# Attention ahead of a mixture of experts on one core: small steps of the attention on another engine in some groups, and another order of its steps

## The chip, the cores and the metric

One Trainium2 chip, one core of it. The metric is the device time of one execution in microseconds. The kernel before took 905.72 us (median of 3 runs, 903.4 to 906.46).

## What is computed

The reference takes q, k and v (8 batches, 12 heads, 448 tokens, 64 wide, fp32), normalizes q and k by their root mean square, and computes attention; its output is laid out as 3584 tokens of 768 and goes through a router and 8 experts of 448 tokens each:

```python
def rmsnorm(x, g):
    rms = np.sqrt(np.mean(x * x, axis=-1, keepdims=True) + 1e-06)
    return x / rms * g
q_n, k_n = (rmsnorm(q, g_q), rmsnorm(k, g_k))
scores = scale * np.matmul(q_n, k_n.transpose(0, 1, 3, 2))
scores = scores - np.max(scores, axis=-1, keepdims=True)
attn = np.exp(scores)
attn = attn / (np.sum(attn, axis=-1, keepdims=True) + 1e-09)
return np.matmul(attn, v)
...
logits = x @ w_gate
...
for e in range(E):
    mask = assigned == e
    h = np.maximum(x[mask] @ w1[e], 0.0)
    out[mask] = h @ w2[e]
```

The experts' part, with the router's choice of 448 tokens for each expert in turn, is not touched by the change.

## The kernel before

The attention works on 24 groups of 4 heads. A group is two pairs of heads; a pair's 448 tokens lie as 7 units of 128 rows (the tails of two heads share a unit). For each group the steps are:

- SyncE's queue loads q, k and v (`load_qk`, `load_v`). ScalarE squares q and k (`square`, L308), VectorE sums the squares (`sumsq`, L320). `rsqrt` makes the inverse root: a logarithm and an exponential on ScalarE (L326, L328), then one correcting step, the **root**, as four small instructions on GpSimd (L331 to L334) or three on VectorE (L337 to L339).
- `norm` (L353) scales k and q by the root, `gain` (L378) multiplies q by the gains. `hi_k` and `hi_q` (L383, L388, ScalarE) take the fp16 part, `lo_k` and `lo_q` (L417, L422) what is left, the **low part**. SyncE's queue turns both by DMA (L429), and `dup_k`, `dup_q` (L397, GpSimd) copy one half to a second tile.
- A first product of q and k (`max_score`, L536 and L539) gives scores from which VectorE takes each row's maximum (`max_reduce`, L550). `put_max` (L555, ScalarE) scales and **shifts the maxima** and puts them down as fp16; TensorE turns them (`tr_max`, L485), ScalarE copies them out (L489, tile mt), and two small DMAs (`row_max`, L496) write them as a row of q's second tile, so that the second product of q and k (`scores`, L569) already has them taken off. ScalarE makes the exponential (`exp`, L580).
- TensorE multiplies by v (`av`, `av_tail`, L604), with the row sums as a 65th column. For each pair VectorE divides (`x_norm`, L639 to L643), ScalarE and VectorE split the result in two fp16 parts (`x_hi`, L654 and L655; `x_lo`, L660 and L661). For batches 0 to 6, TensorE turns a third of it at once (`x_here`, L678) in the same bank of PSUM in which the pair's product stood, and **x's turned copy** leaves it by `x_here_out`, for which `copy` (L371) is called. The gate's products with x follow (`gate`, L741 to L750).

The product tile `po` has two banks, the first scores' ring `pm` one and the ring `psc` two buffers; who holds one keeps the next user waiting.

The order of all these steps is a list. `plan` names 2230 tasks with their engine and what each needs, and `ORDER`, a string of two characters for a task, is the order in which they are written out; each engine then works its own tasks in that order and waits at each for its inputs. Which engine takes a step is looked up by `engine` (L358) in the tables `ENG` and, for the first groups, `FIRST`. Some constants of the router (L1143) and the gate's weights (L187) are made by VectorE in between. A task of the plan that uses the memory port which VectorE and GpSimd have in common is marked so (`port`); in `part`, VectorE's tasks are, except for three names:

```python
port=queue == "D" and name not in ("ss0", "ss1", "put")
```

After the last pair of heads (about 400 us) the router finds the first expert's tokens in a chain of VectorE and TensorE steps, and from about 435 us TensorE multiplies for the experts almost without a gap.

Of the kernel before, what the change touches and what calls it, by code (L numbers as in the profile page):

```python
# [30 lines left out]
AF = mybir.ActivationFunctionType  # L31
OP = mybir.AluOpType
# [57 lines left out]
class Attention:  # L90
# [276 lines left out]
    def copy(self, e, g, o, i):  # L367
        if self.engine(e, g) == "A":
# [442 lines left out]
    def plan(self):  # L811
        plan = Plan(self.RINGS)
        add, P, US = plan.add, self.P, self.US
# [19 lines left out]
        for g in range(self.NG):  # L833
# [20 lines left out]
            for a in self.halves(g):  # L854
# [45 lines left out]
                part("put", "A", "small", self.put_max, after=[("mx", *x), ("c", "qm")], make=("top", *x), opens=[("qm", g)],  # L900
# [3 lines left out]
                add(t + P["trm"], "A", US["small"], self.tr_max, g, 1, after=[("mp", *x)], make=("mt", *x), opens=[("mt", m)],  # L904
# [58 lines left out]
        for pair in range(2 * self.NG):  # L963
# [33 lines left out]
            if b < last and self.HERE:  # L997
                add(s + P["xturn"], "T", 0.12 * len(self.HERE), self.x_here, pair, after=[("x", b, hp)], make=("th", pair), uses=[("xb", b)])
                add(s + P["xtd"], self.engine("xhere", 0), 0.15 + 0.12 * len(self.HERE), self.x_here_out, pair, after=[("th", pair)], make=("xh2", b, hp),
# [17 lines left out]
    def plan_first(self, plan, g, a, t):  # L1017
# [1023 lines left out]
```

## Time and profile before

| what | us |
|---|---|
| median of 3 runs | 905.72 (903.4 to 906.46) |
| the profiled execution's own time | 904.41 |
| its span, first to last instruction | 902.6 |
| TensorE (PE) busy in it | 863.4 |
| VectorE (DVE) busy | 628.0 |
| ScalarE (ACT) busy | 469.2 |
| GpSimd (POOL) busy | 401.6 |

PE is TensorE's matrix product, DVE is VectorE, ACT is ScalarE, POOL is GpSimd, SP is SyncE, whose queue issues most DMAs. A busy share is that of instructions in work; matmuls overlap, so a busy PE can still hide short waits. A wait is put down to the instruction that ended last before it.

### The profile page before, as it was taken

Reading aid. Unit: us, or ns where it says so; the run is one execution under the profiler, and the core shown is the slowest. Engines: PE = TensorE matmul, PEld = TensorE weight load, DVE = VectorE, ACT = ScalarE, POOL = GpSimd, SP = SyncE. Lnnn points to the kernel's source line nnn. Section 1 sums busy time; section 2 is a strip of 40 time slices with the busy share of each in tenths; the row PEclk is TensorE's granted clock in tenths of the full one; section 3 lists DMA queues with packets and bytes.
Section 4 is the critical chain, followed back from the end, with each engine's and each line's share of the span. In section 5 each row is a group of like instructions: output and inputs, shape, how many; then the busy total and the mean of one; then the engine's idle time right before and its main releaser. Section 6 shows DMA issues by size and latency. Waiting matters only on the chain.

```text
span 902.6 us, 27569 instructions
## 1 busy us (share of the span) xinstructions
PE 863.4 (96%) x11763; PEld 557.4 (62%) x11765; DVE 628.0 (70%) x1503; ACT 469.2 (52%) x739; POOL 401.6 (44%) x448
## 2 busy tenths in 40 slices
PE   5989999999999999995999999999999999999996
PEld 2467777677777777784556555565555655555553
DVE  6999888888888988737887776866768675143100
ACT  4987887688887786650434333333333333242110
POOL 7899999889998897202103021101111120200001
PEclk9999999999999999995999999999999999999998
DMA  7677999999899998424747096785929387591001
GB/s 187 145 176 150 195 194 190 207 191 203 193 197 203 174 211 136 118 49 140 259 153 258 28 280 184 207 231 168 278 67 303 114 251 222 169 246 39 27 18 44
DMA packets 253019, 153.64 MB, mean 170 GB/s; under 512 B 178654, under 2 KB 240094, under 8 KB 251872
## 3 DMA queue, kind: packets, MB, share of 16 engines
q1 hardware_dynamic: 247388, 129.39, 60.8%
q0 software_dynamic: 4704, 22.03, 7.3%
q8 instruction: 92, 1.51, 0.7%
q10 hardware_dynamic: 804, 0.46, 0.2%
q14 instruction: 31, 0.25, 0.1%
HBM read 94.43 MB, written 22.02 MB: 129 GB/s over the span
## 4 chain that ended last, share of the span: by engine, by line
PE 66%; issue 18%; DVE 5%; POOL 3%; DMA 3%; ACT 2%; SPq 1%; POOLq 0%; DVEq 0%; ACTq 0%
PE po L604 15%; PE ph L1804 15%; PE py L1821 13%; PE psc L569 12%; PE pm L539 2%; PE py L1830 2%; PE psc L539 1%; DMA qkraw<-in_q_dram 1%; POOL out_dram L1840 1%; DVE mx L550 1%; POOL rows L1737 1%; PE rp L1450 1%; DMA q<-mt 1%; PE pm L536 1%; SPq L249 1%
## 5 line engine op out<-in xcount | busy, mean ns | idle before, releaser
L1804 PE MATMUL ph<-xt,w1h 128*128 128x448 f16 (+2 forms) x804 | 209.5, 344 | 0.0
L604 PEld LDWEIGHTS po<-v,e 128*64 128x64 f32 (+1 forms) x5376 | 172.1, 138 | 41.2 <-issue 20.2
L604 PE MATMUL po<-v,e 128*64 128x65 f32 (+1 forms) x5376 | 185.8, 224 | 2.7 <-DVE xt L371 1.5
L580 ACT ACTIVATE e<-psc 128x896 f32<-128x896 f32 x168 | 151.1, 916 | 57.3 <-PE psc L569 55.8
L1840 POOL DMA_INDIRECT out_dram<-y,idx x32 | 34.3, 1073 | 280.1 <-ACT y L1823 245.7
L569 PE MATMUL psc<-q,k 128*64 128x448 f16 x1344 | 153.5, 354 | 2.1 <-POOL st L333 0.9
L1804 PE MATMUL ph<-xt,w1l 128*128 128x448 f16 (+2 forms) x402 | 135.1, 344 | 0.0
L1821 PE MATMUL py<-w2h,hl 128*128 128x384 f16 x384 | 125.0, 326 | 0.0
L1821 PE MATMUL py<-w2l,hh 128*128 128x384 f16 x384 | 125.0, 326 | 0.0
L1821 PE MATMUL py<-w2h,hh 128*128 128x384 f16 x384 | 125.0, 326 | 0.0
L1804 PEld LDWEIGHTS <-w1h 128*128 128x128 f16 x804 | 74.0, 97 | 63.8 <-issue 2.3
L550 DVE TENSOR_REDUCE mx<-pm 128x2 f32<-128x896 f32 x96 | 104.2, 1085 | 8.4 <-PE pm L539 6.0
L1792 ACT ACTIVATE hh<-ph 128x448 f16<-128x448 f32 x64 | 34.8, 543 | 144.4 <-PE ph L1804 139.6
L1821 PEld LDWEIGHTS <-hh 128*128 128x128 f16 x768 | 73.3, 97 | 46.4
L569 PEld LDWEIGHTS <-k 128*64 128x64 f16 x1344 | 73.6, 110 | 36.8 <-issue 7.5
L1823 ACT ACTIVATE y<-py 128x384 f32<-128x384 f32 x48 | 23.5, 490 | 132.6 <-PE py L1821 104.2
L1737 POOL DMA_INDIRECT rows<-xd,idx x32 | 31.8, 995 | 127.4 <-DVE idx L1631 43.2
L550 DVE TENSOR_REDUCE mx<-psc 128x2 f32<-128x896 f32 (+1 forms) x74 | 77.8, 1058 | 6.5 <-PE psc L539 5.7
L1794 DVE SCALAR_TENSOR_TENSOR hl<-ph,hh 128x448 f16<-128x448 f32 x64 | 39.2, 619 | 60.4 <-ACT hh L1792 60.2
L1724 DVE SCALAR_TENSOR_TENSOR w2l<-stage,w2h 128x768 f16<-128x768 f32 x64 | 60.1, 950 | 22.2 <-ACT w2h L1720 22.1
L1724 DVE SCALAR_TENSOR_TENSOR w1l<-stage,w1h 128x768 f16<-128x768 f32 x64 | 59.4, 950 | 3.3 <-ACT w1h L1720 3.3
L1720 ACT ACTIVATE w1h<-stage 128x1536 f16<-128x1536 f32 x32 | 47.2, 1476 | 21.4 <-DMA stage<-in_moe_w_dram 21.4
(294 smaller groups left out, 1425.3 us busy)
## 6 DMA issues: line engine op xcount, KB each, us to landing
stage<-in_moe_w_dram SPq DMA_DIRECT2D x64, 768.0 KB
vraw<-in_v_dram SPq DMA_DIRECT2D x24, 384.0 KB
xd<-xb SPq DMA_DIRECT2D x8, 1152.0 KB
qkraw<-in_q_dram SPq DMA_DIRECT2D x23, 384.0 KB
qkraw<-in_k_dram SPq DMA_DIRECT2D x23, 384.0 KB
vraw<-in_v_dram SPq DMA_DIRECT2D x24, 64.0 KB
xd<-xm SPq DMA_DIRECT2D x16, 96.0 KB
qkraw<-in_k_dram SPq DMA_DIRECT2D x22, 64.0 KB
```

The lines of the kernel that those rows point to most:

```text
L550: self.nc.vector.tensor_reduce(m, p[:, :k, :448], axis=AX.X, op=OP.max)
L569: nc.tensor.matmul(p[64 * h:64 * h + 64, i, :448], kt[:, a, n + 64 * h:n + 64 * h + 64], qt[:, a, 448 * s:448 * s + 448], start=st, stop=n ...
L580: self.nc.scalar.activation(e, p[:, :, :448], AF.Exp, scale=scale)
L604: self.nc.tensor.matmul(self.po(pair)[64 * n:64 * n + 64, w], self.T["e", d][r, i, q:q + 64], self.v1[g % 2][r, self.slot(a, u, s)], start ...
L1720: self.nc.scalar.activation(h, v, AF.Copy, scale=self.WS)
L1724: self.later(0.93, lambda w=w: self.nc.vector.scalar_tensor_tensor(l[:, w], v[:, w], self.WS, h[:, w], op0=OP.mult, op1=OP.subtract), k, i)
L1737: nc.gpsimd.indirect_dma_start(out=g[:n, c, :], out_offset=None, in_=self.xd, in_offset=bass.IndirectOffsetOnAxis(ap=idx[:n, c:c + 1], axi ...
L1792: nc.scalar.activation(hh, whole, AF.Relu)
L1794: self.later(0.6, lambda: nc.vector.scalar_tensor_tensor(hl, whole, 0.0, hh, op0=OP.max, op1=OP.subtract), k, 3.5, f)
L1804: nc.tensor.matmul(p, a[:, i, c], x[:, b, o], start=j == 0, stop=j == 17)
L1821: nc.tensor.matmul(p, a[:, f, s], b[:, f, o], start=st, stop=sp)
L1840: st = nc.gpsimd.indirect_dma_start(out=self.out, out_offset=bass.IndirectOffsetOnAxis(ap=self.router.idx[k][:n, c:c + 1], axis=0), in_=y[ ...
```

## The change

It gives eight kinds of step an engine of their own group by group: three tables of letters, one letter for each group (`ON`) or pair of heads (`XH`), are asked from group 2 on. D is VectorE, P GpSimd, A ScalarE. Counted from group 2 on: the root is VectorE's in 9 groups (3, 8, 9, 14, 16 to 19, 21), k's norm in 2 (5, 9), the gain in 3 (6, 22, 23), k's low part in 3 (10, 13, 17), q's in 1 (18); all of these were GpSimd's. The shift of the maxima (`put`) is VectorE's in 12 groups and the copy of the turned maxima (`trm`) in 4, both were ScalarE's. x's turned copy is ScalarE's for 25 of 42 pairs, and was VectorE's for all. The numbers of tasks, the buffers and all shapes stay. The order is another one from about the 60th of TensorE's blocks on; up to there it is nearly the same.

```diff
-    ENG = dict(lok="P", loq="P", dupk="P", dupq="P", normk="P", normq="P", gain="P", vfull="A", root="P", xhere="D")
+    ENG = dict(lok="P", loq="P", dupk="P", dupq="P", normk="P", normq="P", gain="P", vfull="A", root="P", put="A", trm="A")
...
+    XH = "AAAAAAAADDAAADDDDADDAADDAADDADAAAAADAAADDDDDDDDD"
+    ON = dict(root="PPPDPPPPDDPPPPDPDDDDPDPP", normk="PPPPPDPPPDPPPPPPPPPPPPPP", gain="PPPPPPDPPPPPPPPPPPPPPPDD", lok="PPPPPPPPPPDPPDPPPDPPPPPP", loq="PPPPPPPPPPPPPPPPPPDPPPPP", put="AAAADADAAADDAADDDADDDDAD", trm="AAAAAAADAAAADAAAADADAAAA")
 
     def engine(self, e, g, a=None):
+        if g >= self.EARLY and e in self.ON:
+            return self.ON[e][g]
...
-            self.nc.scalar.activation(t, self.T.pop(("mp", g)), AF.Copy)
+            self.copy("trm", g, t, self.T.pop(("mp", g)))
...
-        self.nc.scalar.activation(o, i, AF.Copy, scale=-1.0 / self.ROW, bias=math.log(self.PSC) / (scale * self.ROW))
+        m, c = -1.0 / self.ROW, math.log(self.PSC) / (scale * self.ROW)
+        if self.engine("put", g, a) == "D":
+            self.nc.vector.tensor_scalar(o, i, m, c, op0=OP.mult, op1=OP.add)
+        else:
+            self.nc.scalar.activation(o, i, AF.Copy, scale=m, bias=c)
...
-        self.copy("xhere", 0, o, self.T.pop(("th", pair)))
+        self.copy_on(self.XH[pair], o, self.T.pop(("th", pair)))
...
     ORDER = (
-        "020z0o01080706000509030+0-100A0p0q0r04111213141u1t1v1w1x1y2n2r2p2o0w2q2s0x0y3G3F0s0B151T161U1718191V1A1B1C1D"
...
+        "0z11020+120o0-13011008071u0600051t090A030p0q14161v0r04151w1U0B181x171T191y1V1A2n1B1W1C2r1D1E2p1X1F2o1Y1G1Z1K"
...
```

In the new order three places matter for what follows. In the code of the change, lines from 372 on have moved: L371 is L378, L417 L424, L397 L404, L485 L492, L550 L557, L569 L580, L604 L615, L639 to L643 are L650 to L654, L660 and L661 are L671 and L672, L1143 is L1154.

VectorE, at the gate's weights (wg), between the second pair's division and its low parts (xb, xm), which TensorE's turning waits for. Before:

```order
L643 TENSOR_TENSOR po<-po,z 128x7x64
L320 TENSOR_REDUCE st<-sq_134 128x14
L187 SCALAR_TENSOR_TENSOR wg<-wg_123,wg 128x18x8
L660 TENSOR_TENSOR xb<-po,xb 128x2x3x64
L661 TENSOR_TENSOR xm<-po,xm 128x64
```

The same place in the change:

```order
L654 TENSOR_TENSOR po<-po,z 128x7x64
L320 TENSOR_REDUCE st<-sq_134 128x14
L671 TENSOR_TENSOR xb<-po,xb 128x2x3x64
L672 TENSOR_TENSOR xm<-po,xm 128x64
L187 SCALAR_TENSOR_TENSOR wg<-wg_123,wg 128x18x8
L557 TENSOR_REDUCE mx<-pm 128x2
```

The weights went behind the two low parts; a maximum (mx) is now behind them.

VectorE, at the router's constants rankt and rankb, ahead of a turned copy (xt) that frees a bank of `po`. Before:

```order
L660 TENSOR_TENSOR xb<-po,xb 128x2x3x64
L661 TENSOR_TENSOR xm<-po,xm 128x64
L1143 CAST rankt<-rank 128x224
L1143 CAST rankb<-rank 1x8
L371 COPY xt<-po 128x2x128
L320 TENSOR_REDUCE st<-sq_134 128x14
```

In the change:

```order
L378 COPY xt<-po 128x2x128
L1154 CAST rankt<-rank 128x224
L800 TENSOR_TENSOR logits<-po,lsc 128x24
L801 TENSOR_TENSOR logits<-po,lsc 64x8
L557 TENSOR_REDUCE mx<-pm 128x2
L557 TENSOR_REDUCE mx<-psc 128x2 x2
L1154 CAST rankb<-rank 1x8
```

Both constants stand behind a turned copy now, and apart.

GpSimd, at the root of group 8 (st) and the norm of k (kn) that reads it. Before:

```order
L417 TENSOR_TENSOR ks_1841<-kn,ks_1841 128x2x7x64
L397 COPY q_1_129<-q_1347 64x896 x2
L422 TENSOR_TENSOR qs_1869<-qn,qs_1869 128x2x7x64
L331 TENSOR_TENSOR st<-st 128x28
L332 TENSOR_TENSOR st<-st 128x28
L333 TENSOR_SCALAR st<-st 128x28
L334 TENSOR_TENSOR st<-st 128x28
L353 TENSOR_TENSOR kn<-qkraw,st 128x896
```

In the change, where VectorE has that root (L337 to L339):

```order
L404 COPY q_1_129<-q_1452 64x896 x2
L424 TENSOR_TENSOR ks_1721<-kn,ks_1721 128x2x7x64
L353 TENSOR_TENSOR kn<-qkraw,st 128x896
L429 TENSOR_TENSOR qs_1897<-qn,qs_1897 128x2x7x64
L353 TENSOR_TENSOR qn<-qkraw,st 128x896
```

The four small instructions are gone from GpSimd's queue, and k's norm of group 8, which needs VectorE's root, follows a low part directly.

## Rows read from the trace of the kernel before

**Rows 1.** Busy time by stretch, all engines; columns as in its head.
```profile
core 0: us, PE busy (x) PEld busy (x) DVE busy (x) ACT busy (x) POOL busy (x), PEclk, DMA share, GB/s
...
50.00:400.00 350.00, 342.12 (x7572) 255.98 (x7569) 292.16 (x514) 269.03 (x463) 287.80 (x277) 1.00 0.89 176
...
170.62:174.03 3.41, 2.83 (x52) 2.83 (x54) 3.41 (x5) 2.30 (x8) 2.18 (x6) 0.50 1.10 191
```

**Rows 2.** Matmuls' waits, 50 to 400 us: us in total, times, longest us.
```profile
PE po L678 <- DVE xm L661: 2.0, 1, 2.0
PE po L604 <- DVE xt L371: 1.5, 2, 1.3
...
PE psc L569 <- POOL st L333: 0.9, 1, 0.9
```

**Rows 3.** Timeline, 62 to 65 us: start us, us, engine, line, operation.
```profile
62.27 2.09 POOL L378 TENSOR_TENSOR qn<-qn,gg 128x896 f32<-128x896 f32 x1
62.37 2.17 DVE L187 SCALAR_TENSOR_TENSOR wg<-wg,wg 128x144 f16<-128x144 f32 x1
...
64.45 0.55 DVE L660 TENSOR_TENSOR xb<-po,xb 128x384 f16<-128x384 f32 x1
...
65.18 0.30 PE L678 MATMUL po<-ident,xb 128*64 128x128 f16 x4 [2.02 <-DVE xm L661]
```

**Rows 4.** Timeline, 168 to 172 us, VectorE, GpSimd and the next product.
```profile
167.92 2.10 POOL L378 TENSOR_TENSOR qn<-qn,gg 128x896 f32<-128x896 f32 x1
...
168.64 1.51 DVE L1143 CAST rankt<-rank 128x224 bf16<-128x224 f32 x1
...
169.96 1.97 POOL L397 COPY q<-q 64x896 f16<-64x896 f16 x2
170.07 0.88 DVE L1143 CAST rankb<-rank 1x8 bf16<-1x8 f32 x1
...
171.20 0.70 PE L604 MATMUL po<-v,e 128*64 128x65 f32 x8 [1.28 <-DVE xt L371]
```

**Rows 5.** Groups by line and shape, 50 to 398 us: busy us, mean ns.
```profile
L378 POOL TENSOR_TENSOR qn<-qn,gg 128x896 f32<-128x896 f32 x21 | 44.0, 2097 | 1.5
L320 DVE TENSOR_REDUCE st<-sq 128x14 f32<-128x910 f32 x38 | 41.3, 1088 | 0.5 <-ACT sq L308 0.5
...
L417 POOL TENSOR_TENSOR ks<-kn,ks 128x896 f16<-128x896 f32 x21 | 39.8, 1895 | 2.7 <-ACT ks L383 1.6 <-DMA qkraw<-in_k_dram 0.6
...
L353 POOL TENSOR_TENSOR kn<-qkraw,st 128x896 f32<-128x896 f32 x20 | 33.8, 1689 | 1.0
...
L654 ACT ACTIVATE xb<-po 128x384 f16<-128x384 f32 x46 | 22.4, 487 | 6.1 <-DVE po L643 5.8
...
L371 DVE COPY xt<-po 128x256 f16<-128x256 f16 x42 | 11.9, 283 | 9.4 <-PE po L678 8.5 <-PE pm L485 0.7
...
L331 POOL TENSOR_TENSOR st<-st 128x28 f32<-128x28 f32 x20 | 4.7, 233 | 1.3 <-ACT st L328 0.9
```

**Rows 6.** The same view, 0 to 45 us, VectorE alone.
```profile
L339 DVE SCALAR_TENSOR_TENSOR st<-st 128x14 f32<-128x14 f32 x4 | 0.7, 175 | 0.1
```

**Rows 7.** Timeline, 347 to 351 us, VectorE alone.
```profile
348.34 0.86 DVE L1255 TENSOR_SCALAR keyi<-best 128x21 int32<-128x21 int32 x1
...
349.76 0.17 DVE L1257 TENSOR_SCALAR keyi<-keyi 128x21 int32<-128x21 int32 x1
```

**Rows 8.** Timeline, 378 to 383 us, TensorE around the last turning of maxima.
```profile
378.29 0.22 PE L485 MATMUL pm<-ident,qm 128*64 128x128 f16 x1
...
379.85 2.62 PE L604 MATMUL po<-v,e 128*64 128x65 f32 x84
...
382.30 1.49 PE L569 MATMUL psc<-q,k 128*64 128x448 f16 x14
```

**Rows 9.** Timeline, 401 to 437 us, VectorE alone.
```profile
403.62 0.18 DVE L789 TENSOR_TENSOR logits<-po,lsc 128x24 f32<-128x24 f32 x1 [0.64 <-ACT lsc L784]
...
405.92 0.18 DVE L777 COPY logits<-po 128x24 f32<-128x24 f32 x1 [1.38 <-PE po L764]
```

More of the change, by code (lines that the diff above doesn't have):

```diff
@@ L367, in copy, with copy_on @@
     def copy(self, e, g, o, i):
-        if self.engine(e, g) == "A":
+        self.copy_on(self.engine(e, g), o, i)
+    def copy_on(self, queue, o, i):
+        if queue == "A":
             self.nc.scalar.activation(o, i, AF.Copy)
@@ L899, in plan @@
                 m = g
-                part("put", "A", "small", self.put_max, after=[("mx", *x), ("c", "qm")], make=("top", *x), opens=[("qm", g)],
+                part("put", e("put"), "small", self.put_max, after=[("mx", *x), ("c", "qm")], make=("top", *x), opens=[("qm", g)],
                      uses=[("mx", g)])
@@ L903, in plan @@
                     holds=[("pm", ("mp", g))])
-                add(t + P["trm"], "A", US["small"], self.tr_max, g, 1, after=[("mp", *x)], make=("mt", *x), opens=[("mt", m)],
+                add(t + P["trm"], e("trm"), US["small"], self.tr_max, g, 1, after=[("mp", *x)], make=("mt", *x), opens=[("mt", m)],
                     frees=[("mp", g)])
@@ L998, in plan @@
                 add(s + P["xturn"], "T", 0.12 * len(self.HERE), self.x_here, pair, after=[("x", b, hp)], make=("th", pair), uses=[("xb", b)])
-                add(s + P["xtd"], self.engine("xhere", 0), 0.15 + 0.12 * len(self.HERE), self.x_here_out, pair, after=[("th", pair)], make=("xh2", b, hp),
+                add(s + P["xtd"], self.XH[pair], 0.15 + 0.12 * len(self.HERE), self.x_here_out, pair, after=[("th", pair)], make=("xh2", b, hp),
                     opens=[("xt", b)], frees=[("po", pair)])
@@ L1103 @@
-        "RFRERDS2MBMDY3YNYOYPYQYRY4RLRKRMRHRIYKS3RORNRJRGRRRPRSRTRQYWYXYYYLYZYaYBYeYfYgYhYiYDYbYcYSYCXqYlYjYkYTXsXuXt"
-        "XvXwXxYnY5YEYoYpYUYVYMXmXnYdYqYm"
+        "0z11020+120o0-13011008071u0600051t090A030p0q14161v0r04151w1U0B181x171T191y1V1A2n1B1W1C2r1D1E2p1X1F2o1Y1G1Z1K"
+        "0w1a2q1L1c2s1H0x1b1M1J0y1N1+3GCi1i1-3F2M1j1I200sCj2O1z1k21Ck2N2LCm221dCo2P231O1l1e242Q1mCp252t1fCl261hCn272R"
+        "1g1P282v2u1Q2SCq1R1S2T292C2w1r2U3hG+Cr3m2V2DH0G-3k0C2A2W492xH1Cs3jCt2y2aCu3iCw2B2b2E1sCxH23HCv3l2z4A2G2X2k2Y"
@@ new lines @@
+        "2+1nH31o1p1q2-3J2FH43I2ZCy30H6CzH52c310t3KC+D0H732C-ME3nMK2dH833D1MG35H934D2MJD33L3MD42H3N2jHA3o3O2I2lHBD536"
+        "MF3pMI3P2KMH2J3qD6D837S44bD73rHC2e4eS5HDMLD94cMP4B3E3QS6DAHE2mDB3R4CDCHFMQ3SDDMN2fS7MR3s3TDE2g3t3VHG2h2i4DS8"
+        "DF3UDG0uS9MMSAMOHH4dDHDI3D384fDJHI4gMSSB3WHJDKDL3uMUSCDMHKMY3eHLSD3XHM534ESEHO39SFMT3v0v3AMX3BHNSG3CMWDNSHHP"
+        "3wMVDOMZ543xMbDP4hDQ3yMa4FDS3zHQMd4GSIDRHRHS3+3-SJDTHTSKMcDV4jMe4H40HUDUSLHWHV4JSMMfHXDW4ISNHYSO41DXRU5VHZHa"
+        "5XSP4i3Z3d5a3aHc4KSQ3bSRHbMhMg4kSSDY4LMm3Y3cSTMi5+MjHdDZ3fSUMkMl4lSV5ZDa55Db4M5zRVDd4m4N3gMoHeSW0D4PSX4nDcHg"
@@ new lines @@
+        "HfMrSY574ODeDfMpSZMsHhMnSaMt4oMq0ESbHi4QDgScDhHj4pRWDiHk4r5YSd435WMuSeHl4RSfHm485644Mw45HoHn584sMvSgHqSh595A"
+        "HpMz4qSuM+4246SnSvDjHrDkRX47My0FN5Dl4v5BMx5bDmSw4tSxHsDo5C4YN1HtN3SySjHuDnSz4uSlN0HvN4S+Dp5FHwDr5D5dN2DqS-M-"
+        "T04wHyHx4x5cDsHzRYN84XT1DtNC5EH+6PT24TT3N9SkH-4UI05e6QT4NB4S4Z4VN7I1T5Du4WDv5fT6N6T7NA5H5GI2DwSm0G5gRZI35hDx"
+        "T85-5iDyNE5JNG61NIT9DzNH5ID+TAI4E0TB6RNJI55j6uNDTCNF5l4aD-I65KTD5kI8I7TETFTGTHE1I9IAE2TISo5LIBSrTJIC524z60Sq"
+        "6SIDTK4+Sp6U5mTLIE624-6V6TNKIFE34y50E4NN6351NONLE56t64IGSsSi65NQIH5pStE66WRa5nNM666XNP5oNUTME869NSIITNNX67TO"
@@ new lines @@
+        "IJNWE7IKTPIMTQIL687JNR6Y7OINE97KNVEA6Z6vNT5q5MTRIOEBTS6aECIPRbEDIQ5R5rTTISTU7nTV5NIR5O6w5SNcNZTW6b7NNaIT5PNY"
+        "TX5QIU6AEEIVEFNeTdTkNdTlNbEG6c6BEHRc6xEJ7LNg6C6fNiTmEI6DIWIY6yIX6dNhIZTnTaEKToNf6EEMTpIa6eNk0HIbTqIeEL6zNj7M"
+        "Tr6FNl7oTs6gIc7P5TEN0IIdRd5yEO5sNo5U0J6+NnTt5tNrTuIfTvNpNsTw5uIg6-5vTx5wIiIh7Q70NqIjTyEPTzTbEQ6hReNmER6iESNu"
+        "T+NwT-U0IkTcEU71U1NvNyIlETNx6j73Im6GU2EVInEWNz5xU3Nt74EXIo7REYU56kU6IqIpU4EZ72TeIrIsU78D7STfU86MIu6HIt6l8EU9"
+        "6IThTg6J7T6KUAIwTiUBIv0KN+6m75O377EaTj7UIxEbO0N-7p76EcO2Ed6LRfEf8h7rOA7VTYO40LO16NIyEe7W6OOBIzI+UC787qO77XI-"
@@ new lines @@
+        "UDEgUEO80MEiUFO6J07Z7YUGO5J1J2EhUHO9J3UI79J47s8i7b8FEjRgEkJ58HJ67cTZUJOFUK6nJ7UL8GOD6oJ88IUM7a6pOE6rUN6qEl0N"
+        "EmOG7tJ9OCOHEn7dUaOIUbEo8JEpRh7uOJ7vEq7eEr8LOLUcOMEt7wJAUdOPEsUSJBJC7A8KOOJDJEUeEuJF7fJGEvUfURJI0OJH7BUgOK7C"
+        "ON8M7x7DJKJJ6s7EUh8NJLEwUi0PEx7yRi7zOQUQEyJM8O97OTUjJN7+OVUTOS7-OWUk8PEz0QUl7F80OUE-JOUmORUnJP81JQ7gUqUrUoJS"
+        "JRUpUsUU82E+JTUW8RJUUtF0UuJV8SUVF1Uv8jUX7GJWF299UwUYF38lUOOX83F4OZ9C8VOa8m7HOb7hJXOc987iOd8Q7jOYUZ7k8kF5RjF6"
+        "8n8TOe9bJYUxF79B8UOfJZOi9AUyUzF87IJaFAU+8W8oOk8XJb0ROjF9Jc9D8pU-JeJd9EOhV08q0SOgV1FBJfRkFD7m9F8rOrUPOlV2FC7l"
@@ L1105 @@
+        "CCCEXfQpCFXgLnCGGpGqR+CcQvGrGsQsXhQuXiLoXjGuXkQqQtLpQwXlQrLqGtXnXyBqLsLrXzXpR-LtGvX+X-QyY0R0GxY1QxQ-CILwCHGw"
+        "XoR1LuY2GyLvS0GzQzLxR8R3R5Q+L+ChY6CdY7Y8LyCeR7CfR4Y9CgR6LzYAR2Y3L-S1XmM0YFXrYGYHM2M1REYIRBRDM3YJM4RAM5RFR9M6"
+        "XqS2M7RCM8YNYOYPRIM9RJRLYQRKMAYRMCMBRGMDRHYKY4S3YLRMRPYWRTYXYYRSRRYZRNYaRQROYBYeYfYbYgYDXsYhXtYCYiYSYcYUYlY5"
+        "YTYEYjYnYVYkYpYoYdYMYqXuYmXvXwXx"
     )
```

54 lines of the change are left out of this document (15 added, 39 removed).

## The prediction

> **What bounds the kernel now.** I read the busy time by stretch first. Between 50 and 400 us, the attention without its start, TensorE is busy for 342.12 of 350 us, VectorE for 292.16, GpSimd for 287.80 and ScalarE for 269.03 [rows 1]. TensorE's matmuls and weights are the same in number and shape after the change, so what can be won lies in TensorE's 7.9 us without work, and in what the clock costs: for 3.41 us the granted clock is 0.50, the lower of its two levels (1.2 in place of 2.4 GHz) [rows 1]. Moving work off GpSimd wins nothing by itself; it wins only where a matmul waits in the end.
>
> Then the waits. The longest is 2.0 us, for the low part xm; the next 1.5 us, of which 1.3 at once, for a turned copy; then 0.9 us behind a root on GpSimd [rows 2]. The timeline shows why the first two exist. VectorE's step L187, 144 elements wide, took 2.17 us: it began at 62.37, 0.1 us after GpSimd's gain (62.27, 2.09 us), and ended at 64.54, as soon as that had ended; the low parts and the turning queued behind it until 65.18 [rows 3]. The copies rankt and rankb did the same in a row, 1.51 us behind a gain and then 0.88 us behind GpSimd's next copy, and TensorE's product waited for the turned copy until 171.20 [rows 4]. The clock falls at 170.62, inside that very wait (171.20 less 1.28 us). From 400 us on the router and the experts run as before; I take that stretch to shift as a whole.
>
> **What is moved, and its load.** GpSimd gives away 9 roots of four small instructions of 0.23 us (8.4), 2 norms of 1.69 (3.4), 3 gains of 2.10 (6.3), 3 low parts of k and one of q at 1.90 (7.6): 25.7 us [rows 5]. VectorE takes 9 roots of three instructions; half-groups took 0.175 us each there [rows 6], so 4.7 us. Its nine whole-group steps were never run on it in this kernel; the nearest row is a sum over 910 columns, 1.09 us, and GpSimd's 1.69 is the other end: 9 x 1.09 = 9.8 (up to 15). The 12 shifts are as small as an L1257 of 0.17 [rows 7], 2.0 together; the 4 copies of maxima at most the 0.28 of a turned copy, 1.1. It loses 25 turned copies of 0.283, 7.1 [rows 5]. VectorE's load grows by 10.5 us, to 303 of 350. ScalarE takes the 25 copies of 256 columns at 0.28 (VectorE's) to 0.49 us (its own for 384 columns) [rows 5]; I take 0.38, 9.5 us, and it gives 16 small steps away: about 275 of 350. No engine is full by this; what counts is who waits where.
>
> **The terms, against the profiled execution's 904.41 us:**
> - The gate's weights stand behind the low parts in the new order: the wait of 2.0 us ends there, -2.0 (if a low part is late for another reason, 0). Next late is a maximum, which only holds the one buffer of `pm`.
> - The two constants stand behind a turned copy, and not side by side: -1.3 (0 to -1.5).
> - The fall of the clock went with this wait; half of 3.41 us is lost at half clock: -1.7 (0 if another wait takes it down elsewhere).
> - The rest of TensorE's idle time between 50 and 400 us, 7.9 - 2.0 - 1.3 = 4.6 us in small waits. In the new order x's turning stands further behind the last product of its pair and ahead of the next use of its bank, so these should shrink; I take half, -2.3 (0 to -4.6).
> - Last group's maxima. Before, from the turning (378.29, 0.22 us) to the scores that need the row, 14 products, 8 score products and 42 products lie between, and 3.8 us passed until 382.30 with no wait in the rows [rows 8]. In the new order 38 products and six turns of x lie between. 42 products took 2.62 us (84 records, two for each) [rows 8], so 38 take 2.4; four turns of x took 0.30 [rows 3], so six add 0.45. That is 2.9 us, up to 0.9 less than the 3.8 that sufficed: +0.5 (0 to +0.9).
> - The end of the gate. Batch 6's logits were summed at 403.62, 2.3 us ahead of batch 7's at 405.92 [rows 9]; now two of batch 6's gate blocks and its sum come last. The router needs both: +0.8 (0 to +2.3).
> - New waits. By rows 3, 4 and 7 (0.86 against 0.17 us for the same kind), an instruction of VectorE that reads memory as these do stands still while GpSimd finishes. The change adds 30 such steps: 9 roots, 9 whole-group steps, 12 shifts. GpSimd will be busy for (287.8 - 25.7) / 350 = 75% of the time with instructions of about 1.9 us; met at random, a step waits 0.75 x 0.95 = 0.7 us, 21 us in all. The order is not random: as for group 8, the root often stands where GpSimd's next row is the norm that waits for it. I take half, 10 us of VectorE's time, and a quarter of it reaching TensorE, since VectorE has 47 us to spare: +2.5 (0 to +10).
>
> Sum: -2.0 - 1.3 - 1.7 - 2.3 + 0.5 + 0.8 + 2.5 = -3.5, so 900.9 for an execution like the profiled one. That lay 1.3 us below the median of the runs, so I forecast 905.7 - 3.5 = **902.2 us**. By the ends, all gains and no new wait, it is 896.5; with 5 us of new waits and the clock's fall kept, 906.
>
> The Trainium skill's page "SBUF — State Buffer" (section "SBUF: two separate sides") says that GpSimd and a VectorE step with two inputs in SBUF, or one in a mode that uses both ports, take one pair of ports as an exclusive lock, whoever is first keeping it for the whole instruction. The trace agrees: 2.17 us for 144 columns. Its page "VectorE: DVE Perf Modes" (section "Mode 2×_2P — use both read ports for one tensor") lists `tensor_scalar` from SBUF among such; that would be the 12 shifts, which the plan marks as free of the port, and would make them blind hits (12 x 0.7 = 8.4 us on VectorE), while without it they cost their 2.0.
>
> **The rivals.**
> - *The waits only change places (0.28).* A list for engines that are 77 to 98% busy has small waits anywhere; the old ones go, as many come. For it: the three longest waits of before have three different causes [rows 2]. Against: the two largest are removed by plain reordering. Nothing of the gains is kept, the two ends' +1.3 stay: 907.0 (904.5 to 908.4).
> - *The port turns the gain round (0.20).* VectorE's moved steps wait blindly for GpSimd, 21 us, and the low parts, turned copies and maxima behind them are late. For it: of the blocked time in rows 3, 4 and 7 (2.0 + 1.3 + 0.7 + 0.7 = 4.7 us beyond the step's own) TensorE lost 3.3. Against: those steps stood right ahead of something TensorE needed at once. At half, 10.5, less the 5.0 of the first three terms, plus 1.3: 905.7 + 6.8 = 912.5 (908.5 to 917). It decides once most of the moved steps take over twice their own time and TensorE's idle time between 50 and 400 us exceeds 12 us. The lock of the skill's first page is this rival's mechanism.
> - *The forecast (0.52)*: 902.2, in its own range 898.5 to 905.
>
> **How the numbers follow.** 0.3%, 2.7 us, is about what a measurement of this kernel can tell from no change: faster is below 903.0, slower above 908.4. The forecast's case lies below 903.0 in three of four (0.39) and the second case rarely (0.04): faster 0.43. The rest of both, 0.13 and 0.22, and the edge of the third, 0.02: same 0.37. Slower 0.20. The range that leaves out no more than two in ten runs from 898.5 to 910.0, into the lower part of the third case.
>
> **What would show it.** In the changed profile L187, if blocked, has no turning of x behind it, and the longest wait of a matmul between 50 and 400 us is below 1.5 us; idle time there falls from 7.9 to about 5; no stretch at 0.50 before 395 us; the roots L337 to L339 take 0.17 us in most groups, and the shifts (L564) under 0.4 us in the mean; the copy of the last logits, at 405.92 before, comes about 3 us earlier. It is wrong if TensorE's idle time stays at 8 us or more, if a fall of the clock comes elsewhere, or if the moved steps on VectorE last over 1 us in most groups.

## The result, and the profile after

The changed kernel took 909.67 us (median of 8 runs, 908.28 to 915.63) beside 905.1 for the kernel before on the same chip: 1.0068 times as long, 95% interval [1.0047, 1.0088]. Timed a second time it was 1.0049 [1.0031, 1.0066]. So it is slower by 0.5 to 0.7%, where the forecast was faster; 909.67 lies inside the stated range, near its upper end. The profiled execution took 910.4 us, its span 908.6.

First the busy time by stretch, with the columns of [rows 1].

```profile
50.00:400.00 350.00, 335.56 (x7455) 253.57 (x7452) 310.34 (x534) 272.90 (x471) 268.73 (x236) 1.00 0.88 180
224.26:227.67 3.41, 3.41 (x40) 2.73 (x37) 1.19 (x4) 1.98 (x7) 2.38 (x3) 0.50 1.00 241
```

TensorE is now without work for 350 - 335.56 = 14.4 us, where it was 7.9 [rows 1]. VectorE's busy time rose by 18.2 us, not 10.5; GpSimd's fell by 19.1. The lower clock comes elsewhere: at 224.26, right after a wait of 1.7 us for an exponential. In this execution the granted clock was at 0.50 from 20 to 26 us too; a second execution of the same kernel, looked at below, has neither fall.

The matmuls' waits in the same stretch, as in [rows 2]:

```profile
PE pm L546 <- DMA q<-qs: 3.2, 4, 1.5
PE pm L492 <- DVE qm L564: 2.3, 3, 1.6
PE psc L580 <- ACT e L591: 2.2, 2, 1.7
PE psc L580 <- DVE mx L557: 2.0, 2, 1.3
PE pm L492 <- DVE z L652: 1.6, 1, 1.6
```

The two longest of before are gone. New or longer are waits for the shifted maxima (qm L564, a moved step), for maxima (mx, 0.3 us before), for an exponential (0.4 us before) and for q's turning by DMA.

What VectorE's small steps took, one group for each line: smallest, median and largest in ns. (Group 3's root lies ahead of 50 us.)

```profile
L564 DVE TENSOR_SCALAR qm<-mx x12: 167/536/1997, 88.8 to 385.4; 128x14 f16<-128x14 f32 x12
L337 DVE TENSOR_TENSOR st<-st x8: 135/199/910, 109.0 to 310.6; 128x28 f32<-128x28 f32 x8
L338 DVE TENSOR_TENSOR st<-st x8: 186/187/1866, 109.6 to 310.8; 128x28 f32<-128x28 f32 x8
L339 DVE SCALAR_TENSOR_TENSOR st<-st x8: 186/188/1759, 109.9 to 312.7; 128x28 f32<-128x28 f32 x8
L650 DVE TENSOR_SCALAR z<-po x45: 142/155/167, 58.5 to 395.7; 128x7 f32<-128x7 f32 x45
L652 DVE RECIPROCAL z<-z x45: 178/200/203, 59.6 to 395.9; 128x7 f32<-128x7 f32 x45
L654 DVE TENSOR_TENSOR po<-po,z x46: 610/632/633, 50.2 to 396.1; 128x448 f32<-128x448 f32 x46
```

The moved steps (the first four lines) take up to twelve times the shortest of their line (1997 against 167 ns). Nothing else here does: not the reciprocal with one input in SBUF, nor the operation of the shifts when it reads PSUM (L650), nor a product with one input in PSUM (L654).

Now three places in the timeline, all engines, cut to what matters.

```profile
243.62 1.93 POOL L424 TENSOR_TENSOR ks<-kn,ks 128x896 f16<-128x896 f32 x1
243.84 1.76 DVE L339 SCALAR_TENSOR_TENSOR st<-st 128x28 f32<-128x28 f32 x1
...
245.52 0.20 DVE L564 TENSOR_SCALAR qm<-mx 128x14 f16<-128x14 f32 x1
...
245.78 0.24 PE L492 MATMUL pm<-ident,qm 128*64 128x128 f16 x1 [1.60 <-DVE z L652]
...
310.70 1.89 POOL L429 TENSOR_TENSOR qs<-qn,qs 128x896 f16<-128x896 f32 x1
...
310.77 1.87 DVE L338 TENSOR_TENSOR st<-st 128x28 f32<-128x28 f32 x1
...
312.94 1.07 DVE L557 TENSOR_REDUCE mx<-psc 128x2 f32<-128x896 f32 x1
...
314.07 0.38 PE L580 MATMUL psc<-q,k 128*64 128x448 f16 x2 [1.31 <-DVE mx L557]
...
320.26 2.08 POOL L385 TENSOR_TENSOR qn<-qn,gg 128x896 f32<-128x896 f32 x1
320.38 2.00 DVE L564 TENSOR_SCALAR qm<-mx 128x14 f16<-128x14 f32 x1
...
322.44 0.24 PE L492 MATMUL pm<-ident,qm 128*64 128x128 f16 x1 [1.58 <-DVE qm L564]
```

Each time a moved step begins 0.07 to 0.22 us after a long GpSimd instruction and ends with it. At 243.84 it is group 17's root, with group 14's shift queued behind it; at 310.77 group 21's root, with a maximum behind; at 320.38 group 19's shift itself. Each time TensorE waits 1.3 to 1.6 us for what stood behind. (The first is put down to the reciprocal L652, which ended last; the product reads the shift, qm.)

VectorE at the gate's weights, the counterpart of [rows 3], and at the end of the gate, of [rows 9]:

```profile
62.21 0.56 DVE L671 TENSOR_TENSOR xb<-po,xb 128x384 f16<-128x384 f32 x1
62.68 0.21 DVE L672 TENSOR_TENSOR xm<-po,xm 128x64 f16<-128x64 f32 x1
62.81 1.67 DVE L187 SCALAR_TENSOR_TENSOR wg<-wg,wg 128x144 f16<-128x144 f32 x1
...
410.42 0.18 DVE L788 COPY logits<-po 128x24 f32<-128x24 f32 x1 [1.17 <-PE po L775]
...
412.07 0.18 DVE L800 TENSOR_TENSOR logits<-po,lsc 128x24 f32<-128x24 f32 x1 [1.28 <-ACT lsc L795]
```

The weights still take 1.67 us, but with no turning behind them. The last copy of logits comes at 410.42, 4.5 us later than before, and the sum of batch 6 another 1.65 us after it. From that last sum to the end of the span it is 496.5 us (908.6 less 412.07), and before it was 496.7 (902.6 less 405.92): the whole loss lies ahead of the router.

### The profile page after: what moved, and what is told of

Its sections match the earlier page's. It is cut to its first block, busy times and chain, and to the rows that moved or that the text cites. A ratio compares the mean times of both kernels' runs of the same rounds, so it can differ in the third digit from the quotient of the medians.

```text
span 908.6 us, 27571 instructions
## 1 busy us (share of the span) xinstructions
PE 863.1 (95%) x11763; PEld 559.6 (62%) x11765; DVE 648.2 (71%) x1530; ACT 473.8 (52%) x748; POOL 380.8 (42%) x403
## 4 chain that ended last, share of the span: by engine, by line
PE 56%; issue 19%; DVE 12%; DMA 6%; POOL 4%; ACT 1%; SPq 1%; POOLq 0%; DVEq 0%
PE ph L1815 15%; PE py L1832 13%; PE po L615 11%; PE psc L580 8%; DVE mx L557 4%; DMA q<-qs 2%; PE py L1841 2%; DMA k<-ks 2%; PE pm L546 2%; DVE st L320 1%; POOL out_dram L1851 1%; PE psc L546 1%; POOL rows L1748 1%; PE rp L1461 1%; DMA qkraw<-in_q_dram 1%
## 5 line engine op out<-in xcount | busy, mean ns | idle before, releaser
L615 PEld LDWEIGHTS po<-v,e 128*64 128x64 f32 (+1 forms) x5376 | 173.7, 137 | 35.3 <-issue 17.1
L615 PE MATMUL po<-v,e 128*64 128x65 f32 (+1 forms) x5376 | 185.4, 223 | 2.0 <-ACT q L465 1.0
L580 PE MATMUL psc<-q,k 128*64 128x448 f16 x1344 | 155.3, 356 | 4.4 <-ACT e L591 2.2
L557 DVE TENSOR_REDUCE mx<-pm 128x2 f32<-128x896 f32 x96 | 103.7, 1080 | 9.8 <-PE pm L546 8.1
L580 PEld LDWEIGHTS <-k 128*64 128x64 f16 x1344 | 75.1, 110 | 36.4 <-issue 11.1
L557 DVE TENSOR_REDUCE mx<-psc 128x2 f32<-128x896 f32 (+1 forms) x74 | 77.8, 1056 | 3.9 <-PE psc L546 2.8
```

Of the source, the lines that this page charges most:

```text
L557: self.nc.vector.tensor_reduce(m, p[:, :k, :448], axis=AX.X, op=OP.max)
L580: nc.tensor.matmul(p[64 * h:64 * h + 64, i, :448], kt[:, a, n + 64 * h:n + 64 * h + 64], qt[:, a, 448 * s:448 * s + 448], start=st, stop=n ...
L615: self.nc.tensor.matmul(self.po(pair)[64 * n:64 * n + 64, w], self.T["e", d][r, i, q:q + 64], self.v1[g % 2][r, self.slot(a, u, s)], start ...
```

## The experiments

Two theories at the start. **P**, the port: the small steps given to VectorE wait for GpSimd, and TensorE for what queues behind them. **O**, the order: the new order itself puts loads and turnings too near their use. All ratios are to the kernel before, timed beside it; 0.001 is 0.9 us. "Idle" is TensorE's, 50 to 400 us of the profiled execution. The runs were timed in groups on several chips, on which the kernel before took 902.4 to 905.1 us, so runs of different groups are compared by their ratios. An idle time is that of one execution; for "roots back" and "both back" it was the fastest of twelve.

| run | ratio | 95% interval | idle, us |
|---|---|---|---|
| before | 1 | | 7.9, again 6.6 |
| the change | 1.0068, again 1.0049 | [1.0047, 1.0088], [1.0031, 1.0066] | 14.4, again 14.3 |
| new order, old engines | 1.0071 | [1.0046, 1.0097] | 14.6 |
| new engines, old order | 1.0838 | [1.0809, 1.0866] | 56.6 |
| change, shifts back | 1.0004 | [0.9984, 1.0023] | 11.8 |
| change, roots back | 0.9986 | [0.9969, 1.0004] | 8.2 |
| change, both back | 0.9988 | [0.9973, 1.0004] | 8.4 |
| change, wide steps back | 1.0147 | [1.0118, 1.0177] | 20.8 |
| both back, turned copies back | 1.0017 | [1.0004, 1.0030] | 10.4 |
| new order, two gains moved | 1.0015 | [0.9997, 1.0033] | 11.8 |
| both back, idle port steps | 1.0003 | [0.9986, 1.0020] | 9.9 |
| both back, idle reciprocals | 0.9997 | [0.9974, 1.0020] | 9.2 |
| change, three hits out | 1.0012 | [0.9989, 1.0035] | 10.6 |
| change, root of 17 moved | 1.0049 | [1.0026, 1.0072] | 15.5 |
| before, small moves alone | 0.9986 | [0.9972, 1.0000] | 5.2 |
| both back, one DMA earlier | 0.9957 | [0.9942, 0.9973] | 9.7 |

### Order and engines apart

The kernel before with the changed kernel's `ORDER`:

> The new order of the steps, with every step on the engine it had before. Theory P (the port: the steps given to VectorE stand still behind GpSimd's long instructions, and TensorE waits for what queues behind them): without those steps the order's gains stay, up to 5 us as at 215 us of the changed kernel's run, so 900 to 903 us, VectorE's busy time between 50 and 400 us back at 290 to 294 (310 in the changed kernel). Theory O (the order itself puts loads and turnings too close to their use, as the load that ScalarE's square waited 2.4 us for): 907 to 911, as the changed kernel, with TensorE's idle time 50 to 400 us above 12 us.

And the changed kernel with the `ORDER` of before:

> The order of before, with the changed kernel's tables of engines. Theory P: 907 to 913 us, as the same blocked roots and shifts stand in VectorE's row without any gain of the order, VectorE's busy time 50 to 400 us at 305 or more. Theory O: 903 to 907, as before.

The first gave 1.0071, as theory O said; the second 1.0838, far outside both: an order is made for its engines, and each half alone is no measure of its share. Still the first run's trace shows where much of its time went, and it is the port again. Its timeline, 346 to 359 us:

```profile
346.94 2.10 POOL L378 TENSOR_TENSOR qn<-qn,gg 128x896 f32<-128x896 f32 x1
347.02 2.05 DVE L1255 TENSOR_SCALAR keyi<-best 128x21 int32<-128x21 int32 x1
...
351.08 1.95 POOL L422 TENSOR_TENSOR qs<-qn,qs 128x896 f16<-128x896 f32 x1
...
351.19 1.87 DVE L1259 CAST key<-keyi 128x21 f32<-128x21 int32 x1
...
353.10 2.50 DVE L1290 TENSOR_TENSOR cmp<-key,hit 128x672 bf16<-128x672 f32 x1
...
358.10 0.37 PE L678 MATMUL po<-ident,xb 128*64 128x128 f16 x3 [4.64 <-DVE xm L661]
```

The router's early steps, which the changed kernel leaves on VectorE, met GpSimd's last group; the division and low parts stood behind them, TensorE waited 4.64 us, and the clock was at 0.50 after it. A later run moves only the gains of groups 22 and 23 in this kernel:

```diff
     def engine(self, e, g, a=None):
+        if e == "gain" and g >= 22:
+            return "D"
```

> The new order with all engines as before, and of all the moves only the gains of groups 22 and 23 on VectorE, so that GpSimd is done earlier when the router's early steps stand in VectorE's row at 347 us. If the run of the order alone lost its time there (one wait of 5.0 us for xm behind steps that took 2.05, 1.87 and 2.50 us for 0.86, 0.17 and 0.85 of their own, and then 3.4 us at the lower clock): 1.0071 falls by 0.55 to 0.75% to 0.999 to 1.002 of before, and no wait above 2 us is left between 340 and 370 us. If the order lost elsewhere too: 1.004 or more.

1.0015, and no wait of a matmul stands in that window; the same steps took 0.85, 0.17 and 0.85 us there. So that place was most of the loss of the order alone, and the two moved gains were worth about 5 us here. For theory O this leaves at most 3 us, by the interval.

### Roots and shifts

```diff
-put="AAAADADAAADDAADDDADDDDAD"
+put="AAAAAAAAAAAAAAAAAAAAAAAA"
```

> The changed kernel with the 12 shifts of the maxima back on ScalarE, all else as in it. Theory P: the shifts took 0.59 us in the mean for 0.17 of their own, 5 us on VectorE, and one of them 2.00 us with 1.8 us of TensorE's wait behind it: 905 to 908 us (2 to 4 less than the changed kernel's 909.7). Theory O: 909 to 911, no change.

```diff
-root="PPPDPPPPDDPPPPDPDDDDPDPP"
+root="PPPPPPPPPPPPPPPPPPPPPPPP"
```

> The changed kernel with the nine roots back on GpSimd, all else as in it. Theory P: the nine roots took 11.3 us on VectorE for 4.7 of their own, and two of them stand right ahead of waits of 1.8 and 1.5 us of TensorE: 905 to 907.5 us. Theory O: 908 to 911; the same also if GpSimd, with four more small instructions a group, becomes late for the turnings by DMA.

Either alone undoes the loss: 1.0004 (5.8 us less than the first measurement of the change, 4.1 less than the second) and 0.9986 (7.4 and 5.7 us less). Theory P stands, and the new order is not slow as such, since all of it is in both. Both edits together:

> The changed kernel with both the nine roots and the twelve shifts back on their engines of before; the norms, gains, low parts, maxima's copies and turned copies stay moved. If every blocked step charges its own wait, the two gains add (8.0 and 5.3 us less than the changed kernel's 909.7): 896 to 899 us. If the two sets delay one and the same chain, either alone is enough: 901 to 903. If the waits only change places: 904 or more.

0.9988, so the gains don't add. The shifts cost nothing that shows once the roots are gone; in the run without roots their line is

```profile
L564 DVE TENSOR_SCALAR qm<-mx x12: 166/191/958, 88.4 to 374.6; 128x14 f16<-128x14 f32 x12
```

with a median of 191 ns instead of 536. The roots cost little once the shifts are gone, 1.4 us (1.0004 against 0.9988), but not because they collide less: in the run without shifts their lines are

```profile
L338 DVE TENSOR_TENSOR st<-st 128x28 f32<-128x28 f32 x9 | 6.5, 718 | 0.3
L337 DVE TENSOR_TENSOR st<-st 128x28 f32<-128x28 f32 x9 | 4.9, 546 | 0.1
L339 DVE SCALAR_TENSOR_TENSOR st<-st 128x28 f32<-128x28 f32 x9 | 1.7, 187 | 0.3
```

(busy us, mean ns), 13.1 us together, where the change has 11.3. So a microsecond of standing still has no fixed price. That the two kinds cost more together than one by one is shown; why is not.

### The wide steps and the turned copies

Back on GpSimd, in the changed kernel, the 2 norms, 3 gains and 4 low parts:

> The changed kernel with the nine whole-group steps (2 norms, 3 gains, 4 low parts) back on GpSimd; roots and shifts stay on VectorE. Theory P: these nine took 11.6 us on VectorE for nearly 11 of their own by the halves' 0.62 us, so they hardly wait; back on GpSimd its 16 us more make the roots and shifts collide more often: 909 to 913 us. If instead VectorE's load is what costs, 11.6 us less of it: 904 to 907.

1.0147, worse than the change by 7 to 9 us, more than theory P said. The roots on VectorE took 19.2 us in place of 11.3 and the shifts 9.1 in place of 7.1: with more long instructions on GpSimd they stand still longer. So these nine moves are good ones beside the moved roots and shifts. Without those little of it shows: the run after this one, which has all nine, gave 1.0017, and the order alone with two of them (the gains of groups 22 and 23) 1.0015. The turned copies, beside roots and shifts, back on VectorE:

```diff
-XH = "AAAAAAAADDAAADDDDADDAADDAADDADAAAAADAAADDDDDDDDD"
+XH = "DDDDDDDDDDDDDDDDDDDDDDDDDDDDDDDDDDDDDDDDDDDDDDDD"
```

> As the kernel with roots and shifts back, and also all of x's turned copies on VectorE, as before. What then differs from the run of the order alone (910.4) is the nine whole-group steps and four copies of maxima on VectorE. If the turned copies on ScalarE are what the new order needs: 904 to 910. If the order alone lost by the router's early steps, which stood behind GpSimd's gain and low parts of the last group (5 us of one wait and a fall of the clock), the turned copies do not matter: within 2 us of the kernel with roots and shifts back.

1.0017, 2.6 us above the same kernel without this edit. So the copies on ScalarE are worth something too, a little more than the 2 us that the expectation left them: without them matmuls wait for xt L378 8 times, 4.4 us, and with them twice, 0.8.

### The wait at the port by itself

In the kernel with roots and shifts back, idle steps on a tile `d` at the nine places:

```diff
             P.tensor_tensor(y, t, y, op=OP.mult)
+            if g in (3, 8, 9, 14, 16, 17, 18, 19, 21):
+                V, d = self.nc.vector, self.d
+                V.tensor_tensor(d, d, d, op=OP.mult)
+                V.tensor_tensor(d, d, d, op=OP.mult)
+                V.scalar_tensor_tensor(d, d, 0.0, d, op0=OP.add, op1=OP.mult)
```

> The kernel with roots and shifts back, and at the nine places where the changed kernel's VectorE made a root, three idle instructions of the same kinds and size on a tile of their own, on which nothing depends (GpSimd still makes the root itself). Theory P (the wait at the port delays what stands behind in VectorE's row): 4 to 8 us more than the kernel with roots and shifts back (0.9988 of before), so 1.003 to 1.008, the 27 instructions well over 0.3 us in the mean. If the roots cost because their results came late, or by freeing GpSimd: within 1.5 us of it, 0.998 to 1.001.

> The same with three reciprocals of the same 28 columns in place of each three: the one kind of small step on VectorE that reads and writes SBUF and in no trace took longer than 0.20 us. Theory P: 0.20 us each, 5.4 us on VectorE, no wait at the port: within 1.5 us of the kernel with roots and shifts back (0.998 to 1.001). If it is VectorE's load or the three instructions' places as such: as the run with the port's kinds.

The lines of VectorE with the first kind (busy us, mean ns):

```profile
L339 DVE TENSOR_TENSOR d<-d 128x28 f32<-128x28 f32 x9 | 4.5, 504 | 0.0
L340 DVE TENSOR_TENSOR d<-d 128x28 f32<-128x28 f32 x9 | 3.2, 360 | 0.3
L341 DVE SCALAR_TENSOR_TENSOR d<-d 128x28 f32<-128x28 f32 x9 | 1.9, 210 | 0.3
```

and with the second:

```profile
L339 DVE RECIPROCAL d<-d 128x28 f32<-128x28 f32 x27 | 8.7, 321 | 0.6
```

1.0003 and 0.9997: no difference that these intervals show, and the first misses the 1.003 that theory P expected. The reciprocals took 0.32 us, not 0.20, so both kinds loaded VectorE by nearly as much (9.6 and 8.7 us), and the pair doesn't tell the port from the load. The nine idle roots cost 1.4 us, and the nine real ones 1.4 too (1.0004, shifts on ScalarE as here), both hardly more than the intervals can show.

### Single hits

Three hits meant to go out of TensorE's way in the changed kernel: group 17's and 21's roots (moved in `ORDER`) and group 19's shift (on ScalarE).

> The changed kernel with three of its blocked steps taken out of TensorE's way and nothing else: the root of group 17 behind the shift and the division next to it, the root of group 21 behind one maximum, and group 19's shift on ScalarE. In the changed kernel's run they stood ahead of waits of 1.8, 1.5 and 1.8 us. If each wait is a loss by itself: 5 us less than the changed kernel, 1.001 to 1.003 of before. If the collisions are blind and come elsewhere instead: 1.004 to 1.007.

1.0012, in the range expected of separate losses: 3.3 to 5.1 us less than the two measurements of the change. But its trace shows only two of the three gone, those of group 21's root and group 19's shift:

```profile
240.14 1.93 POOL L424 TENSOR_TENSOR ks<-kn,ks 128x896 f16<-128x896 f32 x1
...
240.35 1.76 DVE L339 SCALAR_TENSOR_TENSOR st<-st 128x28 f32<-128x28 f32 x1
...
243.78 0.30 PE L689 MATMUL po<-ident,xb 128*64 128x128 f16 x4 [1.20 <-DVE xm L672]
...
300.47 1.72 DVE L564 TENSOR_SCALAR qm<-mx 128x14 f16<-128x14 f32 x1
...
300.48 1.69 POOL L353 TENSOR_TENSOR qn<-qkraw,st 128x896 f32<-128x896 f32 x1
...
302.25 0.24 PE L492 MATMUL pm<-ident,qm 128*64 128x128 f16 x1 [1.18 <-DVE qm L564]
```

Group 17's root met the same low part, now with x's low parts behind it, and group 18's shift, which took 0.18 us in the change, met a norm. The waits behind such hits were 4.5 us in the change (1.60, 1.31 and 1.58) and are 2.4 here (1.20 and 1.18); the wait of 1.7 us for an exponential is missing too. So the loss goes down as hits are taken away, but the price of one hit is not shown by this run. The first of the three alone:

> The changed kernel with one thing moved: group 17's root behind the shift of group 14 and the division, which stood behind it while it waited 1.76 us for GpSimd. If the wait of 1.8 us of TensorE there is a loss by itself: 1.8 us less than the changed kernel's 1.0068, so 1.004 to 1.006. If it sets off what follows (later hits at 310 and 320 us go with it): 1.003 or less. If it only changes place: 1.0065 or more.

1.0049, the same as the change beside it (1.0049). Its timeline shows why:

```profile
244.49 1.93 POOL L424 TENSOR_TENSOR ks<-kn,ks 128x896 f16<-128x896 f32 x1
244.70 1.76 DVE L339 SCALAR_TENSOR_TENSOR st<-st 128x28 f32<-128x28 f32 x1
...
248.12 0.30 PE L689 MATMUL po<-ident,xb 128*64 128x128 f16 x4 [1.93 <-DVE xm L672]
...
260.26 2.07 POOL L385 TENSOR_TENSOR qn<-qn,gg 128x896 f32<-128x896 f32 x1
...
260.45 1.92 DVE L564 TENSOR_SCALAR qm<-mx 128x14 f16<-128x14 f32 x1
```

The root met the same low part one place further on, as in the run before it, and now x's low parts stood behind it; and group 15's shift, which took 0.62 us in the change, met a gain at 260 us. The wait changed place.

### The two kernels looked at again

> The changed kernel, looked at a second time and timed beside the others. If the three hits are of the kernel's order: roots of 17 and 21 and the shift of group 19 over 1.5 us again, waits of 1.5 to 1.8 us behind them, TensorE's idle time 50 to 400 us above 12 us. If the collisions are a matter of one execution: other places, and fewer than two of the three again. Time: 1.005 to 1.009 of before.

The timeline in the second execution of the change:

```profile
198.54 1.85 DVE L338 TENSOR_TENSOR st<-st 128x28 f32<-128x28 f32 x1
...
202.84 0.95 PE L580 MATMUL psc<-q,k 128*64 128x448 f16 x8 [2.08 <-DVE mx L557]
...
308.43 1.86 DVE L338 TENSOR_TENSOR st<-st 128x28 f32<-128x28 f32 x1
...
318.03 1.98 DVE L564 TENSOR_SCALAR qm<-mx 128x14 f16<-128x14 f32 x1
```

Two of the three hits came again, at 308.43 and 318.03, within 0.02 us in length. At 242 us the root's instructions took 0.18, 0.81 and 0.95 us instead of 0.21, 0.19 and 1.76: nearly the same stretch, cut otherwise. A fourth hit is new, that of group 14's root at 198.54, whose three steps took 0.14 to 0.19 us in the first execution. So most hits belong to the order, and some to one execution.

> The kernel before, looked at a second time. If the waits of 2.0 us (xm, behind the gate's weights) and 1.3 us (turned copy, behind the constants) and the fall of the clock at 170 us are of the kernel: all three again, within 0.5 us in length. If the fall of the clock is of the one execution: the waits again, and no stretch at 0.50 between 50 and 395 us.

Both waits of before came again (2.0 and 1.3 us), and the fall too, at a granted clock of 0.50 from 172 us; a second stretch at 0.50 followed the wait for xm, at 66 us. In the first execution none followed that wait, and in the change's second execution none followed its wait of 2.08 us. So falls came with such waits here, but not with each of them. The small moves alone, in the kernel before:

> The kernel before with three small steps of VectorE moved and nothing else: the gate's weights behind the two low parts and the turned copy, and the two constants rankt and rankb behind the turned copy and behind a later maximum. By the prediction's first three terms (-2.0, -1.3, -1.7): 898 to 900 us, where the kernel before has 903.4 on this chip, no wait of 2.0 us for xm, no fall of the clock at 170 us. If the waits only change places: 902 to 904.

Both waits and both falls are gone from its trace, and the longest wait is 0.8 us. Yet the time is 0.9986: 1.3 us less, by the interval at most 2.5, and not 5. The profiled executions differ by more: their spans are 898.4 us here and 902.6 and 902.1 for the kernel before, on other chips. Of the 29 runs of the kernel before beside this one, those with a mean clock of 0.979 or less took 902.5 to 905.8 us, those at 0.983 or more 900.3 to 903.5. That would fit falls of the clock that not every execution has, but the mean clock doesn't settle it: only two executions of that kernel were looked at, both had the fall at 170 us, and one had a mean of 0.984 and the other 0.979. Why it is 1.3 and not 5 stays open.

### A version that beats both

In the kernel with roots and shifts back, one DMA earlier in SyncE's row:

> The kernel with roots and shifts back, and in SyncE's row group 8's turning of q by DMA ahead of three loads of raw q and k that wait for a buffer. Its landing held TensorE up 1.5 us at 135 us. If that wait is a loss by itself: 1.5 us less than the 0.9988 of that kernel, 0.996 to 0.998. If the loads, now later, take it back: 0.9985 to 1.001.

0.9957 [0.9942, 0.9973], faster than the kernel before by 3.9 us and than the change by more. The wait at 135 us, 1.15 us long in the trace of the kernel it came from, is gone. But the three loads, now later, put off a small DMA of the maxima's row, and TensorE waited 1.9 us for that at 140 us; so the trace does not show why it is faster than the kernel it came from by as much as the ratios say, and their intervals touch.

## Why the prediction was wrong

**The step that failed first** is "a quarter of it reaching TensorE, since VectorE has 47 us to spare". The wait at the port was estimated well: 10 us, and the roots took 11.3 us for 4.7 of their own and the shifts 7.1 for 2.0, 11.7 together. But of this TensorE lost not a quarter: its idle time is 14.4 us with roots and shifts and 8.4 without, 6.0 of 11.7, half; and the time is 5.5 to 7.2 us longer (1.0049 and 1.0068 against 0.9988). The 8.4 is of a fast execution; the 9.7 of the last run, which differs by one DMA, would make it 4.7 of 11.7, two fifths. No one share holds: the roots alone stood still for 8.4 us (13.1 less 4.7) and cost 1.4. Spare time of VectorE elsewhere does not help a shift that TensorE needs at once, and a root costs whatever happens to stand behind it.

**The second** is the sum of the first three gains, -5.0. The two waits are gone as foretold, from the change (no turning behind L187, none behind the constants) and from the kernel with the small moves alone, and there the fall of the clock is gone too. But made alone these moves gave -1.3 (0 to -2.5). The sum was read from one execution, in itself no slow one (904.41 beside a median of 905.1); what it shows did not carry over to the median of many, and why is open. In the changed kernel a fall came back behind another wait: ScalarE's square stood idle for 2.37 us from 218.65 on. Its input comes by a load; the trace names no instruction that it waited for. The same came in two more runs (2.73 us with the shifts back, 2.13 with the root of 17 moved) and not in the second execution of the change; its cause stays open.

**The third**, "I take half" of the rest of TensorE's idle time, -2.3, has no support: with the same order and the roots and shifts back that time is 8.4 us, beside 7.9 and 6.6 before.

The smaller terms: the last maxima cost nothing (foretold +0.5; no wait in the rows there). From the last pair's division to the router's first step it is 7.38 us (404.97 to 412.35), and was 5.84 (400.47 to 406.31): 1.5 more, in the upper part of +0.8 (0 to +2.3). And the low end of the forecast, 896.5, does not come out of its terms: their ends, -2.0, -1.5, -1.7 and -4.6, give 895.9. The wide steps took 11.6 us (foretold 9.8), the turned copies on ScalarE 0.381 us each (0.38).

**The rival that came true** is "the port turns the gain round", by its stated sign: idle time above 12 us (14.4), and most shifts over twice their own time (7 of 12, as well as five of the nine roots taken as a whole). It foretold 912.5, more than the 909.7 measured: it has 21 us of blocked time on 30 steps, where the roots and shifts show 11.7 and the wide steps, which it counted among the blocked, were a gain (1.0147 without them). That 909.67 lies inside the stated range is luck for the forecast's own case, which ended at 905: the range took in the lower part of this rival. Its weight of 0.20 was too low: the waits that the rows of before showed had mostly reached TensorE (3.3 of 4.7 us), and this was set aside as a matter of their place.

The plan marks the shifts as free of the port; they took 0.59 us in the mean from SBUF, and the same operation from PSUM never more than 0.167. The Trainium skill's page "VectorE: DVE Perf Modes" (section "Mode 2×_2P — use both read ports for one tensor") says that `tensor_scalar` can use both ports when it reads SBUF and can't when it reads PSUM, and its page "SBUF — State Buffer" (section "SBUF: two separate sides") that such a step takes the lock: the trace agrees with both.

## What to carry to other kernels

A small step that must wait for another engine's long instruction costs its place in the row, not its own length: look at what stands behind it, and whether the engine that sets the end needs that at once. Here the nine long steps took 11.6 us on VectorE, not far from the 9.8 foretold, and the short ones over twice their own time: the short ones are the ones to be wary of. Price a stall by taking it out alone and timing many runs, not by the one execution that was profiled: here 5.0 us became 1.3.

## What was not expected of the hardware

Two of the hits recur to 0.02 us in separate executions (1.866 and 1.857, 1.997 and 1.984 us). Two moves that cost 1.4 us and nothing by themselves cost 5.5 to 7.2 together. The wait goes both ways: in the kernel with roots and shifts back GpSimd's low part of q at 124.20 took 2.84 us in place of 1.9, begun 0.01 us after a norm of 1.09 us on VectorE. And a reciprocal of 28 columns in SBUF took 0.32 us, where one of 7 took 0.20.
